# mLSTM cell and SwiGLU block on one core: float32 spreads of M and e, weight pieces of 128 columns, the third group's k and q turned on TensorE, and another order of the start

## The chip, the cores and the metric

The kernel runs on one core of one Trainium2 chip. The metric is the device time of the run in microseconds; lower is better.

## What is computed

The inputs are an mLSTM cell (4 batches, 8 heads, 768 steps, head size 40) and the weights of a SwiGLU block; the weights come as float64 and the rest as float32.

```python
for t in range(S):                                   # 768 steps, per batch and head
    m_new = np.maximum(f_gate[:, :, t] + m, i_gate[:, :, t])
    f_stab = np.exp(f_gate[:, :, t] + m - m_new)
    i_stab = np.exp(i_gate[:, :, t] - m_new)
    m = m_new
    C = f_stab * C + i_stab * outer(vt, kt)          # 40 x 40
    n = f_stab * n + i_stab * kt
    denom = np.maximum(np.abs(n . qt), 1.0)
    y[:, :, t] = sigmoid(o_gate[:, :, t]) * (C qt) / denom
x = y.transpose(0, 2, 1, 3).reshape(3072, 320)
g = x @ w_gate                                       # 320 x 1536
out = (g * sigmoid(g) * (x @ w_val)) @ w_out         # 1536 x 320
```

## The kernel before, in words

The sequence is cut into 6 chunks of 128 steps for each batch, 24 chunks in all. Within a chunk the recurrence becomes matmuls: a running sum F of the forget gates, a running maximum M, weights exp(g - M) below the diagonal, scores k q times those weights, and a state C carried from chunk to chunk. Three chunks make a group of 384 tokens, and there are 8 groups. A group's attention output xT (320 features by 384 tokens) feeds its SwiGLU block: 12 hidden steps of 128 features (`hidden`, H in the order lists) and a projection for each of its three chunks (`project`, J). In the steady state, group g's block runs while the attention of group g + 1 is worked out in between.

The engines' work stands in an order written out by hand. Every piece of work is a generator; a string names which generator takes its next step, and `play` walks through the string and afterwards finishes what is left. `START` is the order of the first stretch: the gates, the attention of group 0 and group 1, the weights, and group 0's block. `GROUP` is the order of each later group; group 1 has an order of its own, `GROUP1`. Each engine executes its instructions in the order in which the strings issue them.

The names in START:

- `run`, `tg`, `dec` (L392 to L445, each in two halves A and B): the running sum and maximum with DVE's scans, the turn of g, and the decay between chunks. `mp` and `ep` (`parts`, L433) make the exact parts of M and e.
- `kq`, `v`, `o`, `k`, `x` are transfers; all stand in SP's queue. `store` writes M and e to DRAM, from where `w` and `e` read them back, spread over the partitions, for all chunks but the first three.
- `bar`, `M`, `E` (L486 to L517) spread M and e of the first three chunks over the partitions on PE: `bar` lays a large number above the diagonal into PSUM, `M` adds M[h, t] of a head to all 128 partitions by a matmul with a column of ones, and `E` does it for e.
- `W` (`weigh`, L519): the exponentials on ACT, and v times the weights on POOL. `T` (`turn`, L542): k and q are turned by PE into PSUM and copied out. `S` scores, `N` update of C, `I` and `P` the output within the chunk and from the state before, `F` (`finish`, L627) normalization, output gate and the transposes into xT.
- `R`, `B`, `C`: weights. `R` loads one piece into one of five raw buffers (`NRAW`), `B` loads "behind", the rows 32 to 39 of each head, into the space of h_ring, and `C` (`convert`, L311) makes float32 of the float64 words: two operations on ACT, three on DVE, one on POOL.
- `X` and `x` (L178 to L194): for the later groups k and q are loaded so that DVE turns them with its 32x32 transposes (`turn_x`, `t`), and PE has no part in it.

M and e are held three times by partition group, as bf16 parts that add up to the float32 number exactly: the gates are loaded into partitions 0 to 31, 64 to 95 and 96 to 127, `parts` subtracts the upper halves, and the matrix of ones sums over the three.

Of the kernel before, what the change touches and what calls it, by code (L numbers as in the profile page):

```python
# [19 lines left out]
L = 128  # L20
# [8 lines left out]
GROUP1 = """  # L29
H0*3 o0*2 e0*2 H1*3 o1*2 e1*2 H2*3 o2*2 e2*2 H3*3 k0*2 v0 H4*3 t0*4 H5*3 S0*4 G0*2 t1*4 k1*2 v1 H6*3 S1*4 G1*2 t2*4 H7*3  # L30
x0*8 x1*8 H8*3 S2*4 G2*2 x2*8 x3*8 k2*2 v2 w0 w1 H9*3 H10*3 W0 H11*3 W1 N0*2 N1*2 I0 N2*2 I1 I2 w2 W0*2 P0 P1 P2 F0*2 J0
W1*2 F1*2 W0 J1 F0*3 F2 J2*3 F1*3 F2*4 W2*2 J3 W2 W1 T0*4 T1*4 T2*4 J4 J5*3 W2 J6 J7 J8*3
"""

START = """
R7 pad3 kq0 R7*2 kq0 R7 R2 pad2 R2 pad2 kq0 pad4 R2 pad3 pad0 pad5 R0 bar0 kq0 pad0 pad1 R2 pad4 runA decA tgA R0
mp bar2 R0 M0*2 tgA W0 T0 which decA runB M2 W0 T0 v0 R4 B R0 R4*2 C10 bar1 store C3 decA ep M1 W2 R4 M2 decB T0*2
C10 kq1 tgB kq1 M1 kq1 B W0 C3 decB v2 pad5 N0 C10 B o0 pad1 C6 kq2 W2 N0 B tgB v1 S0 kq1 o0 store kq2 R1 o1 C3 W1
C6 S0*2 decB C6 o2 kq2 R1 C1 T1 o1 R1 o2 W1 R1 decA I0 T1*2 kq2 C0 R6*2 C1 R6 T1 W2 kq3 R6 W1 decA N1*2 C1 C0 N1 w3
kq3 G0 C2 C0 S1 kq5*2 F0 kq5 kq3 kq4 S1 kq5 E1 kq4 R5 G0 S1 G2 kq3 F0 T2 S1 T2*2 C2 P1 F0 R5 G1 F0 N2*2 T2 R10 I1  # L40
N2 G2 C2 F0 G1 R5 S2 B*2 W3 S2 C9 store B H1 R5 S2 H1 E2 W3 F1 S2 B T5*2 W3 F1 P2 I2 F2 decB R10 T3 v3 decB R3 T3*2
H1 F2 R3 F1 C9 T3 F1 F2 C9 T4 F1 T5 R9 T4 T5 R3 R11 e3 R11*2 F2 H0 e3 R10 H0 F2 S3 H0 H3 R10 C7 H3 C7 R3 R11 R9 o3
H4 o4 W3 C7 C5 o3 R9 H3 C13 C5*2 C13 R8 H7 H4 C8 C13 H4 H8 H7 C8 R8 C8 C14 H7 H9 C4 C14 C4 R9 R8 C14 H8 G3 kq4 C15
R8 H8 C15 H10 H9 kq4 C4 w4 S3 R19 C15 C11 R15 w5 H9 C12 H14 C11 o4 H10 S3 H10 S3 T4 C12 P3 H14 C11 W4 e5 C23 I3 G3
o5 H14 v4 C12 F3 W4 N3*2 o5 W5 H2 W4 C23 W4 N3 H2 T4 H13 H2 F3 H5 H13 S4 C19 H13 C19 R13 C23 R12 e5 C17*2 H5 w8 H6
R14 C19 C16 H5 H6 e4 H12 S4 C17 F3 G4 C16*2 C18 e4 w6 R16 H6 C18 S4 W8 C18 W6 H12 H11 S4 C20 F3 R17 H11 H12 C20 H11
C21 S5 R18 C20 C21 J6 C22 v7 W6 C21 P4 C22 v6 W5*2 v5 F3 C22 J0 X J7 k8 S5 w7 G4 I4 v8 X*2 x0 x1 X F4 k7 x3 W7 N4
x3 N4 x1*4 G5 x3 N4 J8 S5 x1 J8 S5 x0 J1 G5 J8 P5 k7 W7 F4 x2 I5 k6 x2*2 J3 x3*2 x1 x3 x0 J4 F5 J2 F4 F5 W7 F4 F5
W8*2 F4 k6 J5 W6 F5 J2*2 J5 W8 k8 J5 W7 x0 x2*3 F5 W6 x2*2 x3*2 x0*3 x1 x0
# [19 lines left out]
def kernel(  # L69
# [51 lines left out]
    PB = {"gen": 4, "cell": NCELL, "conv": NCONV}  # L121
    conv = ctx.enter_context(tc.tile_pool(name="conv", bufs=2))
# [4 lines left out]

    f_sb = gates.tile([128, NB, L], F32)
    i_sb = gates.tile([128, NB, L], F32)
    for c0, c1, quarters in ((0, GC, (0, 2, 3)), (GC, NB, (0,))):  # L130
        for r in quarters:
            for t, a in ((f_sb, f_gate), (i_sb, i_gate)):
                (nc.scalar if r else nc.sync).dma_start(
                    out=t[r * BH:(r + 1) * BH, c0:c1], in_=a.rearrange("b h (c t) -> (b h) c t", t=L)[:, c0:c1])
    for t in (f_sb, i_sb):
        nc.gpsimd.memset(t[BH:2 * BH, 0:GC], 0.0)
# [41 lines left out]
    def place_x():  # L178
        for n in range(4):
            x = conv.tile([128, 2 * NPW], U32, name="raw", bufs=NRAW).bitcast(F32)[:, 0:2 * GC * L]  # L180
            xs.append(x.rearrange("p (j n e) -> p j n e", j=2, e=32))
            nc.gpsimd.memset(xs[n][:, :, :, LO:], 0.0)
            yield
# [51 lines left out]
    wo = {}  # L235
    N4 = 4
    P4 = DF // N4
    WM, WC = 3, DM // 2
    NPW = PR * 128
# [5 lines left out]

    pieces, order = [], []

    def piece(*p):
        order.append(("piece", len(pieces)))
        pieces.append(p)  # L250

    for m in range(NFC):
        if m % NCUT == 0:
            order.append(("behind", m // NCUT))
        if m < 2:
            piece("gv", 0, PR, m * 128, 128)
        elif m % 2 == 0:
            for a in range(0, PR, 2):
                piece("gv", a, 2, m * 128, 256)
    for n in range(2 * (NFC // WM)):  # L260
        piece("out", n // 2 * WM, WM, n % 2 * WC, WC)
    NP = len(order)

    def shape(kind, i):
        return (P4,) if kind == "behind" else (pieces[i][2], pieces[i][4])

    def place(kind, i):
        if kind == "behind":
            return wgv_sb[:, PR, ts(i, P4)]
        which, a, na, c, n = pieces[i]  # L270
        if which == "gv":
            return wgv_sb[:, a:a + na, c:c + n]
        if not wo:

            gates_scope.close()
            wo["sb"] = ctx.enter_context(tc.tile_pool(name="wop", bufs=1)).tile([128, NFC, DM], F32, name="wo_sb")
        return wo["sb"][:, a:a + na, c:c + n]

    def load_behind():

        for c0, c1 in ((0, P4), (P4, DF)):
            for r0, w, f0 in ((0, moe_w_gate, D + 32), (32, moe_w_gate, 32), (HP, moe_w_val, 32),
                              (HP + 32, moe_w_val, D + 32)):
                src = w.rearrange("(x e) f -> e x f", e=X)[f0:f0 + LO, :, c0:c1]
                if plain:
                    nc.sync.dma_start(out=wgv_sb[r0:r0 + 32, PR, c0:c1], in_=src)
                else:
                    nc.sync.dma_start(out=raw4[r0:r0 + 32, 2 * c0:2 * c1], in_=src.bitcast(U32))  # L288
                yield

    def load_piece(i):
        which, a, na, c, n = pieces[i]
        if plain:
            dst = place("piece", i)
        else:
            raw = pst["piece", i] = conv.tile([128, 2 * NPW], U32, name="raw", bufs=NRAW)
            dst = raw[:, 0:2 * na * n].rearrange("p (a d) -> p a d", a=na)
        if which == "gv":
            for r0, w, f0 in ((0, moe_w_gate, 0), (32, moe_w_gate, D), (HP, moe_w_val, D), (HP + 32, moe_w_val, 0)):
                src = w[:, c:c + n].rearrange("(x e) f -> e x f", e=X)[f0:f0 + 32, a:a + na]  # L300
                nc.sync.dma_start(out=dst[r0:r0 + 32], in_=src if plain else src.bitcast(U32))  # L301
                yield
        else:
            src = moe_w_out[a * 128:(a + na) * 128, c:c + n].rearrange("(a p) d -> p a d", p=128)
# [31 lines left out]
    keep = gates.tile([128, NB, L], F32)  # L336
# [14 lines left out]
    ones_of = gates.tile([128, BH], BF16)  # L351
    with nc.allow_low_precision("ones and zeros"):
        nc.vector.reduce_sum(ones_of, ident.rearrange("p (r h) -> p h r", h=BH), axis=AX.X)
    nc.vector.memset(ones_of[BH:2 * BH], 0.0)
# [19 lines left out]
    first, second, third = (list(group(g)) for g in range(3))  # L374
    early = first + second
    F_sb, g_sb, M_sb = f_sb, i_sb, f_sb
    F_end = gates.tile([128, NB, 1], F32)
    m_in = gates.tile([128, NB - 1, 1], F32)
    e_sb = gates.tile([128, NB - 1, L], F32)
# [9 lines left out]
    def rows(c):  # L389
        return slice(0, BH if c else 128)  # L390

    def running(c0, c1):  # L392
        cs = slice(c0, c1)
        F, g, M, f, i, step, end, m = (t[rows(c0)] for t in (F_sb, g_sb, M_sb, f_sb, i_sb, keep, F_end, m_in))
        nc.vector.tensor_tensor_scan(flat(F[:, cs]), flat(step[:, cs]), flat(f[:, cs]), 0.0, op0=ALU.mult, op1=ALU.add)
        nc.vector.tensor_sub(g[:, cs], i[:, cs], F[:, cs])
        nc.vector.tensor_copy(end[:, cs], F[:, cs, L - 1:L])
        nc.vector.memset(step[:, cs], 0.0)
        n0 = max(c0, 1)
        nc.vector.tensor_copy(step[:, n0:c1, 0:1], end[:, n0 - 1:c1 - 1])  # L400
        nc.vector.tensor_tensor_scan(flat(M[:, cs]), flat(step[:, cs]), flat(g[:, cs]),
                                     M[:, c0 - 1, L - 1:L] if c0 else NEG, op0=ALU.add, op1=ALU.max)
        nc.vector.tensor_add(m[:, n0 - 1:c1 - 1], M[:, n0 - 1:c1 - 1, L - 1:L], end[:, n0 - 1:c1 - 1])
        yield

    def decayed(c0, c1):
# [4 lines left out]
        r = rows(c0 - 1)  # L411
        e = e_sb[r, cs]
        nc.vector.tensor_sub(e, m_in[r, cs].to_broadcast([r.stop, n, L]), M_sb[r, c0:c1, :])
        yield
        nc.scalar.activation(e, e, AF.Exp)
        yield
        nc.vector.tensor_tensor(dec_r[:, cs], pair.unsqueeze(1).to_broadcast([BH, n, B * PR]),
                                e_sb[0:BH, cs, L - 1:L].to_broadcast([BH, n, B * PR]), op=ALU.mult)
# [8 lines left out]

    def upper(t):  # L430
        return t.bitcast(BF16).rearrange("p c (t two) -> p c t two", two=2)[:, :, :, 1]

    def parts(t, n):  # L433
        for r in (64, 96):
            x = t[r:128, 0:n]
            nc.vector.tensor_tensor(x, x, upper(x), op=ALU.subtract)
        yield

    def turn_g(c0, c1):
        tp = psum.tile([128, c1 - c0, BH], F32, name="tp_g", tag="cell", bufs=NCELL)  # L440
        for c in range(c0, c1):
            nc.tensor.transpose(tp[:, c - c0, :], g_sb[0:BH, c, :], idb)
# [4 lines left out]
    def store():  # L447
        nc.sync.dma_start(out=M_dram.rearrange("c h t -> h c t")[:, GC:], in_=M_sb[0:BH, GC:])
# [296 lines left out]
    for n in range(4):  # L745
        stream(f"x{n}", load_x, 2, n)
# [85 lines left out]
```

## Time and profile before

| | |
|---|---|
| median of 3 runs | 586.11 us (584.98 to 586.66) |
| the profiled execution | 586.11 us, span 584.3 us |
| PE | busy 564.6 us (97% of the span), 4092 instructions |
| PE's weight loads | 386.0 us (66%) |
| DVE | 316.1 us (54%) |
| ACT | 217.4 us (37%) |
| POOL | 174.1 us (30%) |
| DMA | 51.43 MB, 158385 packets, 136476 of them under 512 B |
| costliest line | hidden matmuls L676, 1980 records, 316.7 us |
| next | projection L695, 552 records, 151.5 us |
| first hidden matmul of group 1 | 121.24 us after the span's start |

A float32 matmul shows as two records and a float32 turn as one. The records of matmuls overlap, since each ends after the next has begun; the cost of a row of them is read from start to start. A share over the whole span is an average: the first 121 us hold the gates, the weights and two groups' attention, the other 463 us are seven groups alike.

### The profile page before, as it was taken

The page shows a single profiled execution, that of the slowest core. Times are in us where ns is not written, and L with a number is a line of the kernel's source. Part 1 is how long each engine was busy: PE and PEld are TensorE (multiplying, and loading weights), DVE is VectorE, ACT ScalarE, POOL GpSimd, SP SyncE. Part 2 cuts the span into 40 slices and gives each one's busy share as a digit, 9 for nine tenths or more (in the row PEclk, how much of TensorE's full clock was granted, in tenths as well). Part 3 has the DMA queues.
Part 4 walks back from the last instruction along what each step waited for, and adds up shares of the span by engine and source line. Part 5 has one row for each costly group of instructions (what it writes and reads, how often), then busy time and mean ns, then how long its engine had stood idle before and what let it go on. Part 6 is the DMA issues. An engine that isn't in the chain of part 4 may idle for free.

```text
span 584.3 us, 10996 instructions
## 1 busy us (share of the span) xinstructions
PE 564.6 (97%) x4092; PEld 386.0 (66%) x4092; DVE 316.1 (54%) x736; ACT 217.4 (37%) x471; POOL 174.1 (30%) x258
## 2 busy tenths in 40 slices
PE   4797999999999999999999999999999999999997
PEld 2676676766776666766677666766677666766666
DVE  8978998626565445624664345634565243633320
ACT  2768789832125313341153222542153321111110
POOL 4564677820216121331125121331125110210000
PEclk9999999999999999999999999999999999999999
DMA  8998997455470566126710465115720300010001
GB/s 175 170 187 185 229 300 187 66 77 105 47 153 11 108 94 129 40 50 111 140 39 11 107 95 119 49 37 105 124 73 12 110 1 2 2 32 2 1 2 34
DMA packets 158385, 51.43 MB, mean 88 GB/s; under 512 B 136476, under 2 KB 150524, under 8 KB 158204
## 3 DMA queue, kind: packets, MB, share of 16 engines
q1 hardware_dynamic: 157948, 50.46, 42.0%
q8 instruction: 32, 0.52, 0.4%
q10 hardware_dynamic: 384, 0.28, 0.2%
q14 instruction: 21, 0.17, 0.1%
HBM read 46.60 MB, written 4.11 MB: 87 GB/s over the span
## 4 chain that ended last, share of the span: by engine, by line
PE 89%; DMA 6%; SPq 4%; issue 0%; POOL 0%; DVE 0%; DVEq 0%; POOLq 0%
PE gv_ps L676 52%; PE o_ps L695 26%; PE yT L581 5%; PE sp L562 3%; DMA raw<-in_moe_w_gate_dram 2%; DMA v<-in_v_dram 2%; PE add L607 2%; SPq L170 2%; SPq L301 1%; PE o_ps L711 1%; DMA M_dram<-f_sb 1%; SPq L288 1%; DMA f_sb<-in_f_gate_dram 0%; SPq L219 0%; SPq L211 0%
## 5 line engine op out<-in xcount | busy, mean ns | idle before, releaser
L676 PE MATMUL gv_ps<-xT,wgv_sb 64*128 64x384 f32 (+2 forms) x1980 | 316.7, 474 | 1.4 <-DVE xT L662 0.9
L676 PEld LDWEIGHTS gv_ps<-xT,wgv_sb 64*128 64x128 f32 x1980 | 190.6, 187 | 115.9 <-issue 2.8
L695 PE MATMUL o_ps<-wo_sb,h_ring 128*128 128x320 f32 x552 | 151.5, 435 | 0.0
L683 DVE TENSOR_TENSOR sg<-sg,gv_ps 128x384 f32<-128x384 f32 x84 | 46.5, 554 | 175.6 <-ACT sg L680 175.6
L680 ACT ACTIVATE sg<-gv_ps 128x384 f32<-128x384 f32 (+2 forms) x99 | 47.5, 480 | 231.5 <-PE gv_ps L676 231.4
L695 PEld LDWEIGHTS o_ps<-wo_sb,h_ring 128*128 128x128 f32 x552 | 104.2, 190 | 43.8 <-issue 1.7
L648 POOL TENSOR_TENSOR yb<-yb,o 128x512 f32<-128x512 f32 x24 | 30.4, 1268 | 96.0 <-DVE yl L647 95.8
L684 DVE TENSOR_TENSOR h_ring<-sg,gv_ps 128x384 f32<-128x384 f32 (+2 forms) x99 | 53.6, 541 | 9.9 <-ACT sg L680 1.2
L533 ACT ACTIVATE w_sb<-w_sb,g_T 128x128 f32<-128x128 f32 x168 | 50.8, 387 | 14.8 <-POOL w_sb L529 14.7
L570 POOL TENSOR_TENSOR qT<-qT,e_bc 128x512 f32<-128x512 f32 x18 | 22.9, 1270 | 108.5 <-PE sp L562 58.9
L529 POOL TENSOR_SCALAR_AFFINE_SELECT w_sb<-w_sb 128x1024 f32<-128x1024 f32 x21 | 22.9, 1092 | 56.6 <-DMA w_sb<-M_dram 55.8
L662 DVE STREAM_TRANSPOSE xT<-yb 128x512 f32<-128x512 f32 x24 | 17.0, 710 | 34.6 <-POOL yb L655 32.1
L655 ACT COPY yb<-yb 32x512 f32<-32x512 f32 x24 | 14.8, 616 | 52.5 <-POOL yb L648 52.2
L562 PEld LDWEIGHTS sp<-qT,kT 64*128 64x128 f32 x384 | 27.7, 200 | 7.6 <-DVE C L624 1.9
L566 DVE TENSOR_TENSOR w_sb<-sp,w_sb 128x512 f32<-128x512 f32 x48 | 31.0, 683 | 2.9 <-PE sp L562 2.1
L227 POOL COPY lo<-o 32x128 f32<-32x128 f32 x48 | 19.3, 402 | 39.3 <-ACT o L224 36.6
L562 PE MATMUL sp<-qT,kT 64*128 64x128 f32 x384 | 28.9, 288 | 1.7 <-DVE C L624 1.7
L581 PE MATMUL yT<-w_sb,v 128*64 128x128 f32 x384 | 28.2, 289 | 0.0
L581 PEld LDWEIGHTS yT<-w_sb,v 128*64 128x64 f32 x384 | 24.3, 144 | 1.0 <-issue 0.8
L700 ACT COPY z_sb<-o_ps 128x320 f32<-128x320 f32 x23 | 9.6, 420 | 36.4 <-issue 20.5
L332 POOL TENSOR_TENSOR wgv_sb<-low,size 128x512 uint32<-128x512 uint32 (+1 forms) x16 | 19.2, 1205 | 9.8 <-DVE size L328 7.4
L635 DVE STREAM_TRANSPOSE yb<-yT 128x256 f32<-128x256 f32 x48 | 18.9, 427 | 5.6 <-PE yT L581 5.4
(100 smaller groups left out, 427.4 us busy)
## 6 DMA issues: line engine op xcount, KB each, us to landing
w_sb<-M_dram SPq DMA_DIRECT2D x21, 512.0 KB
e_bc<-e_dram SPq DMA_DIRECT2D x36, 128.0 KB
k<-in_k_dram SPq DMA_DIRECT2D x48, 80.0 KB
v<-in_v_dram SPq DMA_DIRECT2D x24, 160.0 KB
o<-in_o_gate_dram SPq DMA_DIRECT2D x48, 80.0 KB
raw<-in_moe_w_out_dram SPq DMA_DIRECT2D x8, 480.0 KB
out_dram<-z_sb SPq DMA_DIRECT2D x23, 160.0 KB
raw<-in_moe_w_gate_dram SPq DMA_DIRECT2D x24, 128.0 KB
```

The lines of the kernel that those rows point to most:

```text
L529: nc.gpsimd.affine_select(w, w, compare_op=ALU.is_ge, fill=-NEG, base=0, pattern=[[0, H], [1, L]], channel_multiplier=-1)
L533: nc.scalar.activation(w[:, h], m[h], AF.Exp, bias=g_T[:, c, b * H + h:b * H + h + 1], scale=-1.0)
L562: nc.tensor.matmul(sps[two][:, j, :], lhsT=un["kT"][r, j, :], rhs=un["qT"][r, j, :], start=True, stop=True)
L566: nc.vector.tensor_tensor(w2, un["sp"][two], w2, op=ALU.mult)
L570: (nc.vector if "mb" in un else nc.gpsimd).tensor_tensor(un["qT"], un["qT"], un["e"], op=ALU.mult)
L581: nc.tensor.matmul(un["ys"][two][col * HP:(col + 1) * HP, (h % PR) // 2, :], lhsT=lhsT, rhs=rhs, start=(two, col) in un["fresh"], stop=las ...
L648: nc.gpsimd.tensor_tensor(yb, yb, un["o"].rearrange("p x (four d) -> p x four d", d=D)[:, :, :, 0:32], op=ALU.mult)
L676: nc.tensor.matmul(ps[i][:, cols], lhsT=wgv_sb[r, kc, ts(m, 128)], rhs=xts[g][r, kc, cols], start=(kc == 0), stop=(kc == NKC - 1))
L680: nc.scalar.activation(sg[:, cols], ps[0][:, cols], AF.Sigmoid if g else AF.Silu)
L683: nc.vector.tensor_tensor(sg[:, cols], sg[:, cols], ps[0][:, cols], op=ALU.mult)
L684: nc.vector.tensor_tensor(h_ring[:, (g * NFC + m) % NH, cols], sg[:, cols], ps[1][:, cols], op=ALU.mult)
L695: nc.tensor.matmul(p, lhsT=h_ring[:, (g * NFC + m) % NH, ts(i, 128)], rhs=wo["sb"][:, m, :], start=(m == 0), stop=(m == NFC - 1))
```

## The change

M and e are spread as float32: the matmul takes the column of the identity and M or e itself, on 32 partitions. The gates are then loaded once, by two transfers, and `parts`, `ones_of` and their streams go. The weights for gate and value are loaded in 12 pieces of all rows and 128 columns, where pieces of half the rows and 256 columns stood (but for the first two, which had 128 columns). "Behind" is loaded in four transfers over all its columns instead of eight. The third group's k and q (chunks 6 to 8) are loaded as the first six chunks' are and turned on PE in START; before, they were loaded by `x` and turned on DVE in group 1. `GROUP1` goes, and group 1 is played by `GROUP`. The x buffers are cleared by DVE after START. Of the first six chunks, the update of C takes four DVE operations for each, where POOL made a product and DVE one sum; the two small copies of `den` move from POOL to DVE; and the copies of kT for the first three chunks move from DVE to ACT. The order in START is another one throughout: transfers of k, q, v and o come first, then B, then weight pieces. `project_last`, which makes the last chunk's projection in two column parts with four transfers each on two queues, stands in both kernels.

```diff
+START (its beginning):
+pad0 kq1*2 pad0 bar1 v1 pad1 bar2 kq1 pad2 pad4 kq1 pad4 pad5 pad2 which kq0*2 runA v2 pad1 kq0 o2 T1 pad5 T1 tgA decA kq0 M1 decA
+v0 tgA M1 pad3*2 kq2 runB kq2 T1 T0 kq2 W1 M2 T0 T1 o1 W1 M2 kq2 decB o2 decA S1 B decB W1 decB bar0 W2 B S1 M0 S1 W0 T0 B*2 T0 M0 W0
+o0 S0 o0 o1 R0 W0 W2 S0 R0 W2 G2 S0 decA*2 T2 R0 T2*2 G2 T2 R0 E1 S1 S2 C0 R1 R2 R3 C0 G0 R2 S2 G0 R1 G1 S2 C0 R1 C4 R1 N0 C1 store
+G1 N0 I0 F0 v3 P1 R9*2 N1 R9 F0 E2 R9 kq3 S2 kq3*2 C1 F0*2 kq3 F0 R2 C1 R2 R8 N1 I1 F1 store tgB store H0 kq5 F1 kq5 T3 H0 kq5 tgB P2
...
+START (its end):
+W8 C22 C23 C22 W6 J4 F5 C22 J8 W6 G4 F4 F5 J2 F5 J8*2 F4*2 J5 W6 F4 J2*2 J5 T7*2 T8 J5 T8*3 T6*4
...
-    f_sb = gates.tile([128, NB, L], F32)
...
+    f_sb = gates.tile([BH, NB, L], F32)
+    i_sb = gates.tile([BH, NB, L], F32)
+    nc.sync.dma_start(out=f_sb, in_=f_gate.rearrange("b h (c t) -> (b h) c t", t=L))
+    nc.sync.dma_start(out=i_sb, in_=i_gate.rearrange("b h (c t) -> (b h) c t", t=L))
...
-            nc.gpsimd.memset(xs[n][:, :, :, LO:], 0.0)
-            yield
+            nc.vector.memset(xs[n][:, :, :, LO:], 0.0)
...
-        if m < 2:
-            piece("gv", 0, PR, m * 128, 128)
-        elif m % 2 == 0:
-            for a in range(0, PR, 2):
-                piece("gv", a, 2, m * 128, 256)
-    for n in range(2 * (NFC // WM)):
-        piece("out", n // 2 * WM, WM, n % 2 * WC, WC)
+        order.append(("piece", m))
+    order += [("piece", NFC + n) for n in range(2 * (NFC // WM))]
...
-        for c0, c1 in ((0, P4), (P4, DF)):
...
+        for r0, w, f0 in ((0, moe_w_gate, D + 32), (32, moe_w_gate, 32), (HP, moe_w_val, 32), (HP + 32, moe_w_val, D + 32)):
+            src = w.rearrange("(x e) f -> e x f", e=X)[f0:f0 + LO]
...
-    def parts(t, n):
-        for r in (64, 96):
-            x = t[r:128, 0:n]
-            nc.vector.tensor_tensor(x, x, upper(x), op=ALU.subtract)
-        yield
...
-                nc.tensor.matmul(units[u]["mb"][two][:, j, :], lhsT=ones(h, 128),
-                                 rhs=upper(M_sb)[:, c, :], start=False, stop=True, skip_group_check=True)
+                nc.tensor.matmul(units[u]["mb"][two][:, j, :], lhsT=idb[:, h:h + 1].to_broadcast([BH, 128]),
+                                 rhs=M_sb[:, c, :], start=False, stop=True, skip_group_check=True)
...
-                    nc.tensor.matmul(e[two * DP:(two + 1) * DP, j, :], lhsT=ones(h, DP),
-                                     rhs=upper(e_sb)[:, c - 1, :], start=(j == 0), stop=True, skip_group_check=True)
+                    nc.tensor.matmul(e[two * DP:(two + 1) * DP, j, :], lhsT=idb[:, h:h + 1].to_broadcast([BH, DP]),
+                                     rhs=e_sb[:, c - 1, :], start=(j == 0), stop=True, skip_group_check=True)
...
-            if u in first and name == "k":
-                nc.vector.tensor_copy(un["kT"], tp)
-            else:
-                nc.scalar.copy(un[name + "T"], tp)
+            nc.scalar.copy(un[name + "T"], tp)
...
-            if c > 0 and u in early:
-
-                kept = work.tile([128, PR, D1], F32, name="kept", bufs=1)
-                d = dec[:, c - 1, b * PR:(b + 1) * PR].unsqueeze(2).to_broadcast([128, PR, D1])
-                nc.gpsimd.tensor_tensor(kept, old[:, :, 0:D1], d, op=ALU.mult)
-                yield
-                nc.vector.tensor_tensor(new[:, :, 0:D1], add, kept, op=ALU.add)
-            elif c > 0:
+            if c > 0:
...
-            (nc.gpsimd if u in early else nc.vector).tensor_copy(den[p:p + 32], den[p + 32:p + HP])
+            nc.vector.tensor_copy(den[p:p + 32], den[p + 32:p + HP])
...
-    for u in first + second:
+    for u in first + second + third:
         stream(f"kq{u}", load_kq, u)
         stream(f"T{u}", turn, u, "cell")
-    stream("X", place_x)
-    for n in range(4):
-        stream(f"x{n}", load_x, 2, n)
-    for u in third:
-        stream(f"k{u}", load_k, u)
...
+    place_x()
     for g in range(1, NG):
...
-        if g == 1:
-            for n, u in enumerate(third):
-                stream(f"t{n}", turn_x, u)
-        play(GROUP1 if g == 1 else GROUP, streams)
+        play(GROUP, streams)
```

## The prediction

> **What bounds the kernel now.** I read the page's slices first, then busy time by stage, then the timelines of PE and DVE.
>
> ```profile
> PE   4797999999999999999999999999999999999997
> ...
> DVE  8978998626565445624664345634565243633320
> ...
> PEclk9999999999999999999999999999999999999999
> DMA  8998997455470566126710465115720300010001
> ```
>
> PE is full from the fifth slice on; only the first four, where DVE and the DMA engines are nearly full too, have holes.
>
> ```profile
> 0.00:24.00 24.00, 12.39 (x76) 8.71 (x76) 21.62 (x56) 12.23 (x32) 11.32 (x39) 1.00 0.95 177
> 24.00:41.00 17.00, 15.89 (x124) 12.92 (x126) 13.62 (x29) 11.66 (x20) 11.77 (x20) 1.00 0.95 180
> 41.00:54.08 13.08, 10.07 (x134) 8.33 (x135) 10.85 (x26) 9.73 (x20) 6.49 (x12) 1.00 0.92 191
> 54.08:121.24 67.16, 66.66 (x497) 47.16 (x497) 53.56 (x101) 55.93 (x110) 47.49 (x58) 1.00 0.78 184
> 121.24:187.85 66.61, 66.61 (x488) 46.12 (x488) 34.70 (x87) 18.96 (x42) 15.51 (x22) 1.00 0.46 83
> ```
>
> Columns: stage, its length, busy us of PE, PE's weight loads, DVE, ACT, POOL, then clock, DMA share, GB/s. From 54.08 on PE has no hole. Group 1's first hidden matmul starts at 121.24, and from there one group takes 66.6 us of PE and nothing else decides.
>
> ```profile
> 9.95 1.01 PE L504 MATMUL mb<-f_sb,ones_of 128*128 128x128 bf16 x8 [2.03 <-DMA q<-in_q_dram]
> 10.76 1.05 PE L547 MATMUL tp_kq<-ident,k 128*128 128x128 f32 x4
> 11.61 0.63 PE L504 MATMUL mb<-f_sb,ones_of 128*128 128x128 bf16 x4
> ...
> 21.29 2.23 PE L562 MATMUL sp<-qT,kT 64*128 64x128 f32 x16 [1.70 <-DVE C L624]
> ...
> 40.79 1.29 PE L562 MATMUL sp<-qT,kT 64*128 64x128 f32 x16
> ...
> 54.08 5.88 PE L676 MATMUL gv_ps<-xT,wgv_sb 64*128 64x256 f32 x48 [0.94 <-DVE xT L662]
> ...
> 76.06 0.66 PE L547 MATMUL tp_kq<-ident,q 128*128 128x128 f32 x4
> ```
>
> The 16 score records take 2.23 us at 21 us and 1.29 at 40.8: PE runs at about half speed until some 41 us, which the clock row (9 everywhere) does not tell. At 54.08 PE waits for xT: the stage "group 0's three chunks finished" opens the stretch without holes.
>
> ```profile
> 16.80 0.68 DVE L325 TENSOR_SCALAR bits<-bits 128x512 f32<-128x512 f32 x1
> ...
> 53.31 0.71 DVE L662 STREAM_TRANSPOSE xT<-yb 128x512 f32<-128x512 f32 x1
> ```
>
> DVE converts weights from 16.80 on, between the steps of the attention chunks, and writes the last xT of group 0 at 53.31.
>
> **The sum's frame.** The profiled execution took 586.11 us, 584.3 span and 1.8 around it; it equals the median of the three runs. Everything from 121.24 to the end, 463.06 us, keeps its PE instructions (the projection in two column parts, L705 to 720, is in both kernels). So the new time is 586.1 plus the shift of group 1's start, which is the shift of "group 0's xT is whole" (xT0 below, 54.1) plus the change in what follows it.
>
> **Step 1, the front up to xT0.** *The spread of M* (24 matmuls) turns from bf16 to float32. In bf16 eight cost 0.81 us (9.95 to 10.76). In float32 each is two records, with 32 rows of K. Bounds: the score row, 2.2 us for the 16 records of eight heads, in which two row halves share the array; and the turn row, 0.85/4 = 0.213 us per record of full width, 3.4 us for eight. All heads' weights lie in the same 32 rows, so nothing can share; I take the turn row. *The spread of e* (16): the nearest row is yT, 16 records in 1.91 us (25.78 to 27.69) against 0.60, for each of two chunks. No gain is possible in either: same count, longer form. DVE loses the four subtractions of the parts (1.15 and 0.88 us) and the ones (0.36), and ACT loses four gate DMAs, which cost nothing ahead of its first work at 10.27.
>
> The chain, at the slow PE speed: M of three chunks is scanned at 8.3 (8.07 now). PE: spread of chunk 1, two turns, spread of chunk 2: 3.4 + 1.7 + 3.4 from 8.5, to 17.0; scores 2.2, bar 0.9, spread of chunk 0 with a turn 4.2, scores 2.2: 26.5. DVE's list has no conversion in this time (its next entries are four products with the scores), so from 14.2, where the second scan ends, to 27 it works only on those. In the kernel before, four conversions were started in that time (16.80 first), because SP sent weights from 2.75; now q, k, v and o of three chunks and four transfers with all of "behind" go first, and the first weight piece is the 28th issue, at 13.6 us if each takes the 0.475 us of now. Then decay (0.6), two turns with their ACT copies and the spread of e: DVE's product with e ends near 33. From there DVE's list up to xT0 is: six conversions (2 x 1.68, 4 x 2.08), three finishes of 3.03, their xT 3 x 0.98, eight updates of C 2.0, the rest 3.6: 29.3 us without a hole, with 1.5 of waits (yT, e). xT0 at about 64.
>
> If PE reached full speed near 18, the spread of chunk 0, the scores and both spreads of e would halve: first DVE conversion 28, xT0 at 57.5. PE is unbroken from 13.6 to 21 in the new order, while now it has holes of 0.7 and 1.7 there; but between 24 and 41 it was busy 15.9 of 17 us and stayed slow until the end. I take the middle, 60.8, and keep both ends.
>
> The Trainium skill (TensorE: Matmul & The Clock Gate, Part 1) says that about 3.4 us of sustained matmuls open the clock and an idle window closes it. By that rule the longer spreads would pay for themselves in part, and xT0 would come at 57.5. The trace's 24 to 41 us speaks against it. The same page's closing table says that a matmul with K of 32 takes as long as one with 128, which puts the spread at the dear end; no run here shows that.
>
> **Step 2, from xT0 to group 1.** PE: the 66.66 us of now, less one hidden step of 128 columns (1.2; all three now precede), plus eight turns of four (9 instead of 1; 0.59 each at full speed, 76.06 to 76.65): 70.2. The third group's six were free in group 1, on DVE's 48% of slack; five now stand behind the last projection. ACT, from the copies of that finish (1.7 us before xT0) to the last weight conversion: 8 conversions of 512 at 1.25 (start to start), 8 of 480 at 1.23, one of 384 1.1, 36 exponentials at 0.30, 13 table loads at 1.28, 12 silu 5.5, 3 sigmoids 2.2, 6 copies 3.3: 59.4. Then DVE 2.0, POOL 1.2, the last three parts of the projection 3 x 2.18, the five turns with copies 3.7: 59.4 - 1.7 + 13.4 = 71.1. Both sides end together; with coupling I take 72 (67.2 now). Low end 70.2; high end 77, if ACT has the share of holes that it has now (11 of 67 us).
>
> **Priced at nothing:** pieces of 128 whole rows for 256 half rows: packets of 1,024 bytes took 74 ns on average and those of 2,048 took 151, and there are 12 pieces of 512 either way. C by four DVE operations for one and POOL's, and DVE's den copies, less three kT copies and the parts: +2.7 + 2.0 - 2.1 - 2.4, a wash, and inside DVE's lists above. The memsets of the x buffers, 4 x 0.58 by POOL's row, move to DVE behind the front: covered by group 1 (DVE 34.7 of 66.6), 2.3 without that cover. Group 1's transfers are those of any group; SP issues them while PE has 26 us of hidden steps.
>
> **Where a wait is added:** SP's 51st issue needs a raw buffer that only DVE's second conversion frees, at 37 to 43. Behind it in SP's queue stand the stores of M and e and thus w_sb of the second group (store 5.07 us in the chain of waits), and ACT's exponentials of chunk 3 before the copies of the last finish. That fits before xT0 by 1 to 3 us.
>
> **Sum:** 60.8 + 72 = 132.8 against 121.24: +11.5, so 597.5.
>
> **Rivals.**
> *The front costs little* (12%): PE at full speed from 12 and the spread at the score row's price: xT0 near 55, then 70 to 71: 125 to 126, 590 to 591. For it: unbroken matmuls; against: 24 to 41 us.
> *It is faster* (5%): q, k and v first and no parts let the chunks finish ahead of the conversions. It decides where xT0 comes before 121.24 - 70.2 = 51.0; at 48 the time is 583. Against it: DVE's 29.3 us of listed work would have to start before 20, and PE's spreads alone end at 26.5 or, at full speed, 20.
> *SP's stall runs on* (9%): if w_sb of chunk 3 lands later than ACT's exponentials want it, ACT, DVE and the DMA engines (0.95 busy now, idle in the stall) all slip: 8 us more, 606.
> *As summed* (74%): 591 to 605.
> The same within 0.3% (about what a measurement of this kernel can tell from no change) would need xT0 between 49 and 53: 3%, of which 2 come from the first rival and 1 from the second.
>
> **Range.** Low: 57.5 - 2 (the score row's price) + 70.2 = 125.7: 590.5. High: 64 + 77 = 141: 605.9. It leaves the fast rival and the stall out.
>
> **What would show it.** Right: PE without holes from xT0 on; group 1 from 129 to 137; spreads of 3.4 us per eight heads at the slow speed; DVE with some 10 us of holes between 14 and 27; five turns after the last projection; group 1 still 66.6. Wrong: an xT0 before 55, a hole in PE after group 1's start, or ACT far from full between 60 and 115.

## The result: 605.9 us, and the profile after

The changed kernel takes 605.92 us (median of four, 603.17 to 607.94) against 586.38 for the kernel before on the same chip: a ratio of 1.0334, interval 1.0279 to 1.0389, or 19.5 us more. The profiled execution took 604.03 us with a span of 602.2, which is 17.9 more than before. Two of the four runs (603.17, 604.03) have a mean clock of 0.994, the other two (607.82, 607.94) of 0.986; the profile is of one of the first two.

Slices of the page of the changed kernel, a digit per fortieth of the span:

```profile
PE   7987799999999999999999999999999999999997
...
DVE  7269978973456345563457246553467243632320
...
PEclk9997999999999999999999999999999999999999
DMA  9787899704641167204651267105641200000001
```

PE now has holes in its fifth slice too (7 there, 9 before), DVE is nearly idle in the second (9 before), and the clock row, which held nines throughout, drops to 7 in the fourth slice.

Busy time by stage of the changed kernel (stage, length, busy us of PE, weight loads, DVE, ACT, POOL, clock, DMA share, GB/s):

```profile
0.00:24.00 24.00, 20.02 (x87) 15.74 (x88) 12.91 (x40) 8.54 (x23) 7.77 (x34) 1.00 0.94 161
24.00:39.40 15.40, 14.04 (x110) 11.81 (x109) 6.45 (x13) 9.94 (x20) 4.87 (x9) 1.00 1.14 164
39.40:64.91 25.51, 16.13 (x198) 13.73 (x190) 23.52 (x60) 14.47 (x27) 13.29 (x15) 0.87 0.66 141
64.91:139.30 74.39, 72.26 (x508) 49.72 (x509) 60.64 (x118) 66.90 (x124) 44.23 (x47) 1.00 0.72 163
139.30:205.90 66.60, 66.60 (x489) 44.82 (x488) 33.98 (x84) 21.73 (x50) 16.08 (x22) 1.00 0.37 73
```

The stage from xT0 to group 1 starts at 64.91 (54.08 before) and is 74.4 us long (67.2). Group 1 starts at 139.30 (121.24): 18.1 us later. A group's stage is 66.60 us, as before, and the span grew by 17.9, so all the loss lies ahead of group 1: 10.8 in the front, 7.2 behind it.

Timeline of PE in the changed kernel (start, duration, line, operation; in brackets the idle time before it and what ended it):

```profile
7.40 3.77 PE L443 MATMUL mb<-f_sb,ident 32*128 32x128 f32 x16 [0.92 <-DVE f_sb L358]
...
16.72 2.08 PE L498 MATMUL sp<-qT,kT 64*128 64x128 f32 x16
...
24.74 2.08 PE L498 MATMUL sp<-qT,kT 64*128 64x128 f32 x16
...
30.17 1.97 PE L454 MATMUL e_ps<-e_sb,ident 32*64 32x128 f32 x16
...
45.82 2.16 PE L605 MATMUL gv_ps<-xT,wgv_sb 64*128 64x128 f32 x20 [2.97 <-DVE C L549]
...
56.30 4.23 PE L605 MATMUL gv_ps<-xT,wgv_sb 64*128 64x128 f32 x40 [2.82 <-POOL wgv_sb L297]
60.33 1.09 PE L498 MATMUL sp<-qT,kT 64*128 64x128 f32 x16
64.91 4.59 PE L605 MATMUL gv_ps<-xT,wgv_sb 64*128 64x256 f32 x40 [3.48 <-DVE xT L591]
```

The 16 records of eight heads of M take 3.77 us and those of e 1.97. The scores take 2.08 at 16.72 and at 24.74 and 1.09 at 60.33: half speed in the first two. Three holes of 2.8 to 3.5 us stand ahead of the two rows of early hidden steps and of xT0.

Timeline of DVE in the changed kernel:

```profile
15.62 0.50 DVE L372 TENSOR_TENSOR dec_r<-pair,e_sb 32x48 f32<-32x48 f32 x1 [3.10 <-ACT e_sb L370]
18.89 1.29 DVE L502 TENSOR_TENSOR w_sb<-sp,w_sb 128x512 f32<-128x512 f32 x2 [2.77 <-PE sp L498]
26.92 1.29 DVE L502 TENSOR_TENSOR w_sb<-sp,w_sb 128x512 f32<-128x512 f32 x2 [6.74 <-PE sp L498]
...
32.18 0.69 DVE L506 TENSOR_TENSOR qT<-qT,e_ps 128x512 f32<-128x512 f32 x1 [3.65 <-PE e_ps L454]
32.79 0.56 DVE L290 TENSOR_SCALAR bits<-bits 128x384 f32<-128x384 f32 x1
...
64.14 0.71 DVE L591 STREAM_TRANSPOSE xT<-yb 128x512 f32<-128x512 f32 x1 [0.38 <-ACT yb L584]
```

DVE waits 12.6 us in three holes between 12.5 and 26.9, and its first weight conversion stands at 32.79 (16.80 before).

Busy time and granted clock of the changed kernel (columns as above), from 8.7 us on:

```profile
8.70:25.76 17.06, 17.06 (x83) 14.44 (x83) 5.42 (x12) 7.16 (x24) 0.75 (x1) 1.00 0.93 178
```

and in three stretches behind xT of chunk 0:

```profile
46.24:49.66 3.42, 3.42 (x37) 2.87 (x34) 3.17 (x11) 0.86 (x2) 0.87 (x1) 0.50 0.65 118
49.66:56.48 6.82, 3.89 (x52) 2.99 (x49) 6.20 (x15) 4.83 (x9) 3.55 (x5) 1.00 0.69 177
56.48:59.90 3.42, 3.42 (x33) 3.37 (x34) 3.28 (x8) 2.30 (x5) 2.32 (x2) 0.50 1.07 199
```

The row of 8.70 must be read with the timeline: PE was busy all of these 17.06 us, the column says 1.00, and yet the scores in it took 2.08 us. The trace's record of the clock only begins when full speed is first granted (39.4 here, 41.1 before); what lies ahead of it is shown as 1.00 and ran at half speed. Afterwards it shows, behind each of the two holes of some 2.9 us, a clock of 0.50 for 3.4 us. In this execution these two stretches are all (2 x 3.4/2 = 3.4 us, 0.6% of the span, so 0.994).

The two runs with 0.986 are 4.3 us longer and left no trace. The mean clock alone doesn't explain them: half speed ahead of the first grant is not in it, and of the five runs with PE kept busy (below) the fastest, 604.45, has 0.986 and the other four 0.992 to 0.994. What may have happened is seen in another run with this order, the early conversion below. There the clock fell at the hole ahead of xT0 as well (0.50 from 63.40 to 70.22):

```profile
64.65 7.32 PE L605 MATMUL gv_ps<-xT,wgv_sb 64*128 64x256 f32 x40 [3.48 <-DVE xT L591]
```

These 40 records took 4.59 us in the changed kernel's profile, 2.7 less, behind a hole of the same 3.48 us.

### The profile page after: what moved, and what is told of

Read it like the earlier page. It is cut to its first block, busy times and chain, and to the rows that moved or that the text cites. A ratio compares the mean times of both kernels' runs of the same rounds, so it can differ in the third digit from the quotient of the medians.

```text
span 602.2 us, 11062 instructions
## 1 busy us (share of the span) xinstructions
PE 581.8 (97%) x4156; PEld 398.0 (66%) x4156; DVE 316.1 (53%) x743; ACT 227.9 (38%) x484; POOL 167.2 (28%) x236
## 4 chain that ended last, share of the span: by engine, by line
PE 84%; DMA 5%; DVE 4%; POOL 2%; SPq 2%; ACT 2%; issue 1%; POOLq 0%; DVEq 0%; ACTq 0%
PE gv_ps L605 47%; PE o_ps L624 22%; PE yT L517 5%; PE sp L498 4%; PE add L543 2%; PE mb L443 2%; DMA raw<-in_moe_w_gate_dram 2%; PE tp_kq L486 1%; DMA k<-in_k_dram 1%; PE o_ps L640 1%; POOL wo_sb L297 1%; DMA v<-in_v_dram 1%; DMA out_dram<-z_sb 1%; SPq L194 1%; DMA q<-in_q_dram 1%
## 5 line engine op out<-in xcount | busy, mean ns | idle before, releaser
L605 PE MATMUL gv_ps<-xT,wgv_sb 64*128 64x384 f32 (+2 forms) x1980 | 321.0, 478 | 10.0 <-DVE xT L591 3.5
```

The source lines that it names most:

```text
L605: nc.tensor.matmul(ps[i][:, cols], lhsT=wgv_sb[r, kc, ts(m, 128)], rhs=xts[g][r, kc, cols], start=(kc == 0), stop=(kc == NKC - 1))
```

## The experiments

Each is compared with runs of the kernel before on the same chip, which had a median of 585.2 to 585.7 in the three groups. "xT0" below is the start of the first hidden step of 256 columns in the profiled execution, and the date of full speed is where that execution's clock record begins.

### The spreads and the order, each alone

**The parts put back into the new order.** In the changed kernel:

```diff
-  lhsT=idb[:, h:h + 1].to_broadcast([BH, 128]), rhs=M_sb[:, c, :]
+  lhsT=ones(h, 128), rhs=upper(M_sb)[:, c, :]          # e likewise; gates on four row blocks
-START: ... tgA decA kq0 M1 ... runB kq2 ...
+START: ... tgA decA mp kq0 M1 ... runB ep kq2 ...
```

> The changed kernel in its own order, with the three bf16 parts of M and e put back (gates on four row blocks, ones, four subtractions; the spreads are bf16 again). Theory A (the float32 spreads on a slow PE made the front late): eight heads of M fall from 3.7 to about 0.85 us and those of e from 2.0 to 0.6, PE's chain ends some 9 us earlier, xT0 moves from 64.9 to 56-58 and the time is 596-599. Theory B (the order made it late: q, k, v first, weights asked for 10 us later): DVE still has nothing to convert until the pieces land, xT0 stays at 62-64 and the time at 602-605.

Measured: 600.57 us, ratio 1.0248 (1.0218 to 1.0279): some 0.86% or 5 us came back, between the two theories. xT0 is at 60.02, 4.9 earlier. What the shorter spreads saved was partly lost again: PE now had holes throughout, and the clock was at half speed in several stretches up to 65.6 us.

**The float32 spreads put into the old order.** In the kernel before: the same diff backwards, with `mp` and `ep` dropped from its START.

> The kernel before in its own order, with only the spreads of M and e in float32 (no parts, no ones, gates loaded once). Theory A: PE was busy 15.9 of 17 us from 24 to 41, so some 8.5 us more of M and 2.8 of e on PE put xT0 from 54.1 to 60-63 and the time to 592-595. Theory B: under 2 us, 586-588, as DVE has conversions to do meanwhile and PE's holes of 1.7 to 2.7 us before 24 us take a part.

Measured: 587.36 us, ratio 1.0026 (1.0009 to 1.0044). Theory B's time: 1.5 us, though by the expectation's sum PE had some 11 us more to do. Of the twelve runs ten took 586.62 to 588.18 us and two 584.65 and 584.66, and the profile is of one of these two. In it the float32 spreads filled PE's holes, and full speed came earlier (31.77 for 41.09): the turn at 35.95 took 0.66 us, while in the kernel before the one at 35.48 took 1.12. xT0 was at 53.78 against 54.08. So the profile shows how the longer spreads can cost nothing; where the other ten runs lose 2 to 3.5 us against it, no trace shows.

**The old order given to the new code.**

```diff
-START = <the list of the changed kernel>
+START = <the list of the kernel before without mp, ep, X; its x and k6..k8 places hold kq6..kq8;
+         C4/C5 and C12/C13 change names, as the pieces are numbered differently> T6*4 T7*4 T8*4
```

> The changed kernel's code with the order of the kernel before: its list up to group 1 with the parts left out, the third group's q and k loaded in the places of the x transfers, and that group's turns at the end of the list. Theory A: the float32 spreads are still there, so xT0 is at 60-63 and group 1 starts 5 us later still for the turns: 597-600. Theory B: xT0 is back at 54-56 and only the turns remain: 591-593.

Measured: 598.41 us, ratio 1.0218 (1.0192 to 1.0245), xT0 at 62.99. The time is theory A's, but the experiment before had just shown that the spreads cost only 1.5 in this order. Up to 30 us its PE timeline is that of the old order with float32 spreads; then comes this line:

```profile
32.93 1.09 PE L499 MATMUL tp_kq<-ident,q 128*128 128x128 f32 x4 [2.48 <-DMA q<-in_q_dram]
```

In its place in the old order four whole transfers of the weights "behind" carry twice the bytes of the halves ahead of this q. Something priced at nothing was at work; two more runs take it apart.

**The same with the eight half transfers.**

```diff
-for r0, w, f0 in (...): src = ...[f0:f0 + LO]                       # 4 transfers
+for c0, c1 in ((0, P4), (P4, DF)): for r0, w, f0 in (...): src = ...[f0:f0 + LO, :, c0:c1]   # 8
```

> The changed kernel's code in the old order, but with the weights behind loaded in the eight half transfers of the kernel before in place of four whole ones. With whole ones the first four carry twice the bytes ahead of q of chunk 2 and PE waited 2.48 us for that q at 30.4. Theory C (the whole transfers made it late): q is there in time, xT0 goes back from 63.0 to 54-56 and the time from 598.4 to 590-592, which is before plus the spreads' 2.2 and the turns' 3.8. Theory D (it is the moved small work: C by four operations on DVE, the den copies on DVE, kT on ACT): xT0 stays at 61-63, 597-599.

Measured: 596.35, ratio 1.0177 (1.0157 to 1.0196), xT0 at 60.46. The wait for q is gone, 2.4 us came back, not the 6 to 8 of theory C. DVE's timeline of this run shows the next wait:

```profile
32.99 0.76 DVE L564 SCALAR_TENSOR_TENSOR C<-C,dec,add 128x41 f32<-128x41 f32 x4 [3.08 <-PE add L558]
33.67 0.56 DVE L305 TENSOR_SCALAR bits<-bits 128x384 f32<-128x384 f32 x1
```

**And with the update of C in the addition's place.**

```diff
 if c > 0:
+    if u in first + second: yield      # the update moves to the third of the three old places
     for j in range(PR): nc.vector.scalar_tensor_tensor(new[:, j, 0:D1], ...)
```

> The version with the old order and the half transfers, with one thing more: DVE's update of C (now four operations) stands in DVE's list where the addition stood, behind the conversion, in place of where POOL's product stood; there DVE waited 3.08 us for PE with a conversion behind it. If that place is the rest of the loss: xT0 56-57 and 591-593, the sum of the spreads (2.2) and the turns (3.8). If the operations themselves cost it (C by DVE, den by DVE, kT by ACT): 595-597.

Measured: 593.86, ratio 1.0144 (1.0127 to 1.0162), xT0 at 57.96: 1.9 us back, between the two theories. Of the 8.4 that remain, 1.5 are the spreads and 3.6 the turns (next), if these cost here what each costs alone; 3.3 are left for the rest: C, den and kT on other engines, pieces of 128 columns, the memsets. No run separates these.

The clock is a rival for part of these terms: in the three runs full speed came at 49.12, 43.76 and 43.44, against 41.09 in the kernel before. Whether an edit cost its wait or the later clock behind it, no run shows.

**The third group turned, alone, in the kernel before.**

```diff
-START: ... X k6..k8 x0..x3 ...            +START: ... kq6..kq8 ... T6*4 T7*4 T8*4
-play(GROUP1 if g == 1 else GROUP, streams)
+play(GROUP, streams)
+place_x()                                 # the x buffers are cleared behind START
```

> The kernel before, with only the third group loaded as q and k and turned on PE (all three chunks, six records, behind the last projection) instead of through the x buffers and DVE in group 1. The front keeps xT0 at 54.1. PE gets six turns of 0.59 and waits for ACT's copies between them, with nothing else to do there: 3.5 to 4.5 us, 589.6-590.6. If those turns were hidden beside other work the time would stay 586; if ACT's copies, not PE, set them, six of 0.66 and the holes between: 5 us, 591.

Measured: 588.93, ratio 1.0062 (1.0044 to 1.0081), so 3.6 us, as expected. PE's timeline, the first turn and the hidden step behind the last:

```profile
119.80 0.60 PE L540 MATMUL tp_kq<-ident,k 128*128 128x128 f32 x4
...
123.49 6.72 PE L669 MATMUL gv_ps<-xT,wgv_sb 64*128 64x384 f32 x40
```

Six turns in 3.69 us, with nothing beside them.

### What decides in the new order

**The wait of SP's queue taken away.**

```diff
-START: ... C4 R1 N0 C1 store G1 ... kq3 S2 kq3*2 C1 F0*2 ...
+START: ... C4 R1 N0 C1*2 store G1 ... kq3 S2 kq3*2 F0*2 ...
```

> The changed kernel with one step moved: DVE's part of the second weight conversion goes ahead of the first update of C (from 42.2 to about 35.4 us), so that the raw buffer that SP's 51st issue waits for from 38.1 to 44.4 is free by 38. Theory E (that stall of the queue is what the stretch after xT0 pays for; DMA was at 0.25 then): the weights and the second group's q, k, v land 4 to 6 us earlier, group 1 starts 3 to 6 us earlier, 599-603. Theory F (DVE's list up to xT0 decides, and the stall only fills a gap): within 1.5 us of the changed kernel, 604-607; xT of chunk 0 comes 2 us later.

Measured: 606.40, ratio 1.0363 (1.0338 to 1.0388): nothing, theory F's time. xT of chunk 0, which theory F put 2 us later, came 0.6 earlier (43.67 for 44.24), so DVE's list is not shown to be the reason.

**Two weight pieces first, converted in DVE's holes.**

```diff
-START: ... decA S1 B decB ... M0 W0 o0 S0 o0 o1 R0 W0 ...
+START: ... decA S1 R0*4 R1*4 o0*2 o1 B decB ... M0 C1 W0 C1 C2 S0 W0 C2 C1 C2 ...
```

> The changed kernel with two weight pieces (eight transfers, 1 MB) put ahead of the weights behind in SP's queue, and their conversions in DVE's holes between 14 and 27 us, ahead of chunk 0's products with the scores; the PE order is untouched. Theory G (DVE's late start on the conversions is the loss in the front: six conversions stand between the products and the last xT): two of 2.08 us leave that list, xT0 goes from 64.9 to 60-61, the raw buffers come free earlier, group 1 starts 4 to 6 us earlier: 600-602. Theory H (PE's chain of spreads and the clock decide, DVE has room): xT0 stays within 1 us, 604-607. If the weights behind, now 1 MB later, hold up the first conversion of them: slower than 607.

Measured: 607.82, ratio 1.0372 (1.0352 to 1.0392). The two conversions stood at 24 to 28.7 and delayed the products with the scores by 1.7 us; afterwards DVE had 4.2 us less to do, and still the last xT came at 65.41 instead of 64.14. Theory G in its plain form falls: DVE's list does not decide what happens between 32 and 65 us. The chain of waits of the changed kernel says what ended last there (start, duration, what):

```profile
52.02 0.64 ACT bits L287
...
54.98 1.27 POOL wgv_sb L297
...
56.30 4.25 PE gv_ps L605 x40
60.55 0.26 ACT sg L609
...
60.82 1.28 ACT L472
62.12 0.86 ACT w_sb L472 x3
...
63.42 0.62 ACT yb L584
...
64.14 0.27 DVE xT L591
```

It runs through ACT's queue, which keeps its order: a conversion at 52.02 that stands behind the copies of chunk 1's finish, the early hidden steps that need this weight, their silu, a table load, chunk 3's exponentials, and only then the copies of chunk 2's finish. ACT was busy 14.47 of 25.51 us in this stage. No run moved an entry of this queue, so the chain is read from the trace and not shown by an experiment.

Both experiments also show where SP's queue stands next. The longest waits of that queue in one stretch (30 to 60 us in the changed kernel, 38 to 56 in the two others; us in total, times, longest), from the changed kernel:

```profile
SPq L265 <- DVE size L293: 7.2, 2, 6.3
SPq L146 <- PE add L543: 2.9, 1, 2.9
```

from the early conversion:

```profile
SPq L146 <- PE add L543: 6.9, 1, 6.9
```

and from the two weights first:

```profile
SPq L146 <- PE add L543: 9.8, 1, 9.8
```

The transfer that waits at L146 is the first k of the third group's last chunk (`kq8`). It needs the ring slot of chunk 2's k, which PE's `add` of that chunk frees near 50. Behind it in the queue stand the second group's w_sb and e_bc and the weights. Take 6 us of waiting from the raw buffer, and the queue waits 4 to 7 us longer for this slot: it goes on at 50.55, 50.01 and 50.74. In the version with 128 rows below it went on at 43.79, and group 1 started 4.2 us earlier; but there the clock opened earlier too, and xT0 came 6.6 us earlier. That moving `kq8` back would bring this time home was not tried.

**PE kept busy in the holes.**

```diff
 ps = [psum.tile([128, TW], F32, name="gv_ps", tag="gen") for _ in range(2)]
+if g == 0 and m < 2 and i1 == 1:
+    for n in range(10): nc.tensor.matmul(ps[0], lhsT=ident_b, rhs=late (three times), start=True, stop=True)
```

> The changed kernel with ten bf16 matmuls of 384 columns, whose sums are thrown away, ahead of each of the first two hidden steps of 128 columns, where PE stood idle for 2.97 and 2.82 us. If these holes are what brings half speed back for 3.4 us each time, the clock stays at full speed from 39 us on. Theory I (the fall-backs lie on the path): up to 1.7 us each come back, and the runs lose their spread: 602-604. Theory J (DVE's list decides between 32 and 65): no more than 1 us, 604-607.

Measured: 606.78, ratio 1.0362 (1.0340 to 1.0384): no gain, and runs still from 604.45 to 608.19. It does not test theory I well: the first ten ran at 40.4 to 42.2 and left a hole of 1.23, but the list has the third early step ahead of the second, so the second ten stood behind one that waits for its weight; a hole of 2.47 remained at 51, the clock fell there, and once more after the hole of 3.51 ahead of xT0. The profile is of the fastest run, in which the clock happened to open at 20.30: the first early step starts 2.4 us earlier than in the changed kernel (43.44 for 45.82) and the second 2.7 (53.56 for 56.30). Then the second ten take 3.06 us, ACT stands 2.69 us for the step behind them, and xT0 comes only 0.9 earlier, at 64.03. So the added matmuls spent what the clock had won. What full speed throughout would be worth stays open.

### The clock

**Spreads over 128 rows, in both orders.** The rows below the 32 hold zeros:

```diff
+nc.gpsimd.memset(f_sb[32:128, 0:GC], 0.0)                # e likewise
-lhsT=idb[:, h:h + 1].to_broadcast([BH, 128]), rhs=M_sb[:, c, :]
+lhsT=ident[:, h:h + 1].to_broadcast([128, 128]), rhs=f_all[:, c, :]
```

> The changed kernel with its float32 spreads over 128 rows in place of 32: M and e get rows of zeros below their 32, and the weights are the whole column of the identity, so that the sums are the same. If a record takes as long with 128 rows as with 32 and the clock follows busy time alone, nothing changes: PE was busy without a hole from 8.7 to 25.8 and stayed at half speed, 604-608. If the clock follows how much of the array is at work (32 rows of 128 count as little), full speed comes at 12-16 us instead of 39.4, PE's chain up to the first conversion shortens by 6 to 9 us, and the time is 596-601. If a record's time grows with the rows, the chain grows by over 10 us: above 615.

> The kernel before in its own order with float32 spreads over 128 rows. If the clock follows the share of the array that works, it opens at 12-15 us instead of 31.8 (32 rows) or 41 (bf16), the front shortens by 3 to 5 us, and the time is 580-584, below the kernel before. If busy time alone counts, it equals the version with 32 rows: 585-588.

Measured: 599.85 in the new order, ratio 1.0232 (1.0209 to 1.0256), so some 6 us less than the changed kernel, and 584.94 in the old one, 0.9980 (0.9964 to 0.9996). PE's timeline and two stretches of the clock in the new order:

```profile
7.38 3.76 PE L449 MATMUL mb<-f_sb,ident 128*128 128x128 f32 x16 [0.75 <-POOL v L324]
...
12.59 1.95 PE L449 MATMUL mb<-f_sb,ident 128*128 128x128 f32 x16
```

```profile
12.55:22.79 10.24, 8.23 (x81) 7.35 (x80) 3.15 (x6) 9.14 (x27) 2.25 (x3) 1.00 0.83 204
22.79:33.03 10.24, 9.48 (x84) 7.55 (x82) 5.32 (x12) 5.61 (x11) 3.39 (x7) 0.50 0.93 169
```

The first 16 records took 3.76 us with 128 rows and 3.77 with 32: a record's time is the same with 32 rows and with 128. But full speed came at 12.55 instead of 39.4 (9.74 in the old order), and the next sixteen took 1.95. Then half speed came back at 22.79, behind 3.4 us in which PE was half idle, with a longest hole of 1.44 at 20.

In the new order xT0 came at 58.32, 6.6 us earlier, and group 1 at 135.10, 4.2 earlier: the clock fell once more at xT0. In the old order xT0 came at 49.78, 4.3 us earlier than in the kernel before, but group 1 at 119.51, only 1.7 earlier. Behind xT0 PE now waits for POOL's conversion of a weight:

```profile
49.78 6.54 PE L651 MATMUL gv_ps<-xT,wgv_sb 64*128 64x256 f32 x48 [0.93 <-DVE xT L637]
58.00 9.29 PE L651 MATMUL gv_ps<-xT,wgv_sb 64*128 64x384 f32 x54 [1.68 <-POOL wgv_sb L327]
```

So an earlier xT0 is worth less here than its own shift, since the weights are not ready for it.

**The best version.** The old order with 128 rows, and one swap on DVE:

```diff
-START: ... W1 C6 S0*2 decB C6 ...
+START: ... W1 S0*2 C6 decB C6 ...
```

> The kernel before with float32 spreads over 128 rows (584.94, clock open from 9.7 to 20.0 us and again from 33.6), and DVE's products of the second chunk's scores ahead of a weight conversion in place of behind it, since PE stood 2.35 us for them at 18.9 and the clock fell there. If the shorter hole keeps the clock open: 580-583. If it falls all the same: 584-586.

Measured: 584.37, ratio 0.9980 (0.9965 to 0.9996). The hole at 18.9 shrank from 2.35 to 0.69 us, and the clock fell all the same, at 20.06, behind 3.4 us with no hole above 0.83; another hole of 2.86 opened only afterwards, at 22.8, where PE waits for DVE's copy of dec. xT0 is at 51.46, later than without the swap, and group 1 at 119.74, about the same. So the kernel before with float32 spreads over 128 rows is at best 0.2% faster: both versions have the ratio 0.998 with an interval that just leaves out 1, which is less than the 0.3% that the prediction called measurable.

### Where the 19.5 us are

By the ratios, times 586: spreads 1.5 (in the old order), turns 3.6, the small moves 3.3, the place of C's update 1.9, the whole transfers 2.4: 12.7, the time of the new code in the old order. The other 6.8 are the new order, with an interval of some 3.5 on either side, since the changed kernel's own runs scatter. The terms depend on each other: the spreads that cost 1.5 in the old order cost 5 in the new one. By stages of the profiled executions the new order adds 1.9 us ahead of xT0 (64.91 for 62.99) and 3.4 behind it (74.39 for 70.97).

## Why the prediction was right, and where its steps failed

The direction and the place held: the loss is ahead of group 1, in the front and in the stretch behind it, and nothing after it. The mechanism held in part: the slow spreads and the turns are there, but 7.6 of the 19.5 us, by the terms above, come from what was priced at nothing. The size was 597.5 for 605.9, 11.5 us for 19.5. That is outside the band of 591 to 605 which had 74%, and at the very end of the stated range, 605.9. That it lies there is luck: the end was made of a front of 64 and a stretch of 77, and they were 64.9 and 74.4. Of the prediction's own signs two failed, group 1 between 129 and 137 and PE without holes from xT0 on. Against the profiled run, group 1 was put at 132.8 and stood at 139.30, 4.1 us of it in the front (60.8 for 64.9) and 2.4 behind (72 for 74.4).

**The spreads' price** was 3.4 and 1.91, measured 3.71 (7.40 to 11.11) and 1.89 (30.17 to 32.06) from start to start: the first a tenth short, the second right. By the second rule of the Trainium skill that the prediction named (TensorE: Matmul & The Clock Gate, the closing table: K of 32 takes as long as K of 128) it had to be the dear end; the runs with 128 rows now show it: 3.76 against 3.77.

**PE's chain** was to end at 26.5 and DVE's product with e to end near 33: 26.8 and 32.9. DVE's holes between 14 and 27 were to be some 10 us: 12.6 from 12.5 on. These steps stand, except that the first weight piece was issued at 17.06 instead of 13.6.

**"I take the middle, 60.8"** is the step that failed in the front. The cold end, 64, was near the time, 64.9. The middle gave weight to full speed near 18 us, for PE was to be unbroken; it was (17.06 of 17.06 us from 8.70), and the clock did not open until 39.4. The skill's Part 1 rule, read as a rule on busy time, speaks for 57.5, and this run is against it. The run with 128 rows says what such a reading leaves out: with spreads as long and all rows in use the clock opened at 12.55, and xT0 came at 58.32, near the prediction's other end.

**"DVE's list up to xT0: 29.3 us"** gave the right number for the wrong reason. DVE was that busy (28.49 of 32.73 us from 32.18 on), but with 4.2 us less on its list, begun 1.7 later, the last xT still came 1.3 later. The chain through ACT's queue (the copies behind chunk 3's exponentials, which the prediction had seen and thought to fit) ends at the same date; that it decides is read from the trace.

**Step 2.** PE's sum was 70.2, and PE was busy 72.26: the turns' records cost what was said, the hidden steps 1.8 us more than those before. Five turns stood behind the last projection, in 3.2 us. The rest, 2.1, is idle time. ACT, the other side that was to end together with PE, was busy 66.90 of the 74.39 us. PE did not stay without holes, as the text had it for the case of being right: the largest, 0.70 inside the projection, ends with POOL's conversion of a weight, another of 0.40 with ACT's silu. That the conversions run late because SP's queue stood until 50.55 is read from the queue's waits and the run with 128 rows, not shown by itself.

**Where a wait is added:** the 51st issue stood from 38.1 to 44.4 (37 to 43 was said), and taking it away won nothing. The prediction did not go on to the next waiting entry of the same queue, the third group's k behind PE's `add`. With the first wait gone the second takes its place.

**Priced at nothing:** the wash was none. In the old order the whole transfers cost 2.4, the earlier place of C's update 1.9 and the small moves 3.3. The packets were priced by bytes and time in total; those of 1,024 bytes took 79 ns on average in the changed kernel, near the 74 of before, but what the narrower pieces cost by themselves no run shows. What was not priced is which bytes go ahead of a q that PE waits for.

**The rivals.** "The front costs little" and "faster" are out: xT0 was 64.9. "SP's stall runs on" named 606, and 605.9 was measured, but the wait it meant is not the cause: without that stall the time is 606.4. The queue then stands as long for its next entry, so that its standing costs nothing at all is not shown.

## What to carry to other kernels

When a wait in an in-order queue is priced, look up the next entry of that queue that waits, and the one after: taking one away moves the time only if none of the others stands at the same date. A sum of one engine's work that hits the measured date is no proof that this engine decides; follow the last link (here the copy ahead of xT) back through the queue it stands in. And two orders of the same instructions price one edit differently (1.5 and 5 us here), so an edit that comes with a new order is to be tried in the old one as well. Before a profile is read for the reason of a median, see where its execution lies among the runs: here one was of two outliers and another of the fastest.

## What was not expected of the hardware

The clock does not follow PE's busy time alone. In the changed kernel spreads over 32 rows kept PE busy for 17 us without a hole and left it at half speed until 39.4; in two more executions of this order full speed came at 39.50 and 41.61. The same over 128 rows, as long per record, had it at 12.55, and at 9.74 and 9.82 in the old order, where with 32 rows it came at 31.77 to 49.12. The rows are not all, either. In the run with PE kept busy, with identical instructions up to 40 us and 32 rows, it came at 20.30, and the spread of four heads at 21.6 took 1.15 us for 2.07 in the changed kernel (22.74).

What closes it is not the length of a hole alone. In the changed kernel holes of 2.97 and 2.82 us brought half speed back for 3.4 us each, and one of 3.48 ahead of xT0 did not, though holes of the same length did in the early conversion and with 128 rows; in the old order with 128 rows and the swap, it fell behind holes of 0.83 and 0.69. From the first grant to the last fall, the stretches in the clock records are 3.41 us or whole multiples of it, in every run. So the clock dates of one execution are not a property of its order alone.
